# Two pieces of the last x sums formed two half parts later, two blocks of output sums held aside, all products of half part 1 ahead of its tiles

## The chip, the core and the metric

The kernel runs on one core of a Trainium2 chip. The metric is the device time of one execution in microseconds (us). Five engines run side by side and wait for one another by semaphores: TensorE (PE, with its weight loads shown as PEld), VectorE (DVE), ScalarE (ACT), GpSimd (POOL) and SyncE (SP), which here issues all DMA transfers in its program order. Each engine executes its instructions in order.

## What is computed

```python
attn_out = _attn_ref(**attn_kwargs)
x = np.ascontiguousarray(attn_out.transpose(0, 2, 1, 3)).reshape(B * S, H * D)
x = _moe_ref(x=x, **moe_kwargs)
return _moe2_ref(x=x, **moe2_kwargs)

def _moe2_ref(x, w_in, w_out):          # x 2304 x 512, w_in 512 x 2048, w_out 2048 x 512
    h = x @ w_in
    g = np.where(h > 0.0, h, np.exp(np.minimum(h, 0.0)) - 1.0)
    return (g @ w_out).astype(np.float32)
```

An attention with local windows and global tokens feeds a mixture of eight experts, all of which run on all tokens and are weighted by a Sinkhorn-normalised gate. Its output x feeds a last network of two layers with an ELU between them. The change lies where the experts end and the last network begins.

## The kernel before

**Numbers.** Each fp32 operand is held as a high part and a low part (names ending in h and l, or hh and hl for the hidden values). One product of two operands is three matmuls: high by high, low by high, high by low.

**Token groups.** The 2304 tokens go through the experts in two groups, p = 0 (1024 tokens) and p = 1, and through the last network in the same two groups, there called p = 2 and p = 3. The nine blocks `accs[0]` to `accs[8]` (128 x 512 fp32 each) collect the expert output of a group. For the first group they are stored and read back early. For the second group they still hold the expert output when the last network begins, and from then on `part2` uses the same blocks for the outputs of the last network.

**Layer one** is done with seven products instead of eight (Strassen's scheme in Winograd's form). Its operands on the x side are four blocks and four sums of blocks, called 11, 12, 22, s1 to s4 here. `x_pair(p, j, rows)` forms them for a piece j of a group: TensorE transposes two blocks of `accs` into two PSUM tiles x2t (`turned`), ScalarE and VectorE form high and low parts (`hi`, `lo`, with four stores to the scratch tensors xo3h and xo3l), then the sums (`first`, `second`) and their high and low parts (`hi_sums`, `lo_sums`, with two more stores). For the second group there are five pieces, formed in the order 1, 0, 2, 3, 4. Piece j reads `accs[j]` and `accs[j + 4]`, piece 4 only `accs[8]` and is half as large. The tiles for the high and low parts have the tags s1, u2 and u3, each with two buffers that are used in turn.

**The same tags serve the products.** `Quad.product` runs one of the seven products (1 to 7); a product is six matmuls. Products 1, 6 and 7 keep a partial result in SBUF under the tags s1 (ScalarE copy, L1064), u2 and u3 (VectorE add, L1066). Products 2, 3, 4 and 5 end in `evac` (VectorE add, t, L1018) and then `elu`: three ScalarE activations (L1036 to L1038), two VectorE operations (eg, L1041 and L1042), a ScalarE cast that gives the high part hh (L1054) and a GpSimd subtraction that gives the low part hl (L1055). Product 3 is accumulated into the PSUM bank of product 5 of the same half part after that bank has been read.

**Half parts.** The last network runs in 16 half parts, eight for each group, called 0 to 15 here. Each has the products of one half of a 512-wide piece of the hidden layer, mixed with the tiles of layer two of the half part before. A tile (`part2`, also six matmuls, two per low or high part of each of two hidden chunks) adds to one block of `accs`. The order inside a half part is a string: a1 is product 1 of quad a, b1 of quad b, z3 product 3 of the half part before, t4 tile 4 of the half part before. Half part 0 runs `TURN_0`, 1 runs `TURN_1`, 2 to 7 run `TURN_A`, 8 (where the group changes) runs `TURN_AB`. Tiles 4 to 7 of a half part need the results of its products 5 and 4, tiles 0 to 3 those of its products 2 and 3.

**What sets the order.** The scheduler is off, so program order is issue order on each engine. `side2` is a queue of small steps; a fixed number (`per`) is taken from it after every tile of the experts' last part (`mix2_all`) or every element of a half part's string. Before the change the last part of the experts takes pieces 1, 0 and 2 from it, five steps after each tile, and half part 0 takes pieces 3 and 4, three steps after each product. Between the two, `layer_two(0, f)` issues eight loads of the layer-two weights (w2h, w2l), which wait until the experts' last tile has read the old ones. `layer_one` loads the weights wh and wl.

**Raw tiles.** `raw_tile` gives one of four large SBUF buffers in turn; each piece of the x sums takes two (xsr, xsh).

Of the kernel before, what the change touches and what calls it, by code (L numbers as in the profile page):

```python
# [47 lines left out]
XUSE = ("11", "s2", "12", "s3", "s1", "22")  # L48
W22 = ("11", "t2", "21", "t3", "t1", "t4", "22")
TURN_0 = "a1 a6 a2 a7 a5 a4"  # L50
TURN_1 = "a1 a6 a2 z3 a7 t4 a5 t5 a4 t6 t7 t0 t1 t2 t3"
TURN_A = "a1 a6 t4 a2 t5 z3 t6 a7 t7 a5 a4 t0 t1 t2 t3"
TURN_AB = "a1 a6 t4 a2 t5 z3 t6 a7 a5 t7 a4 b1 t0 b6 b2 t1 a3 t2 b7 t3 b5 b4"
TURN_B = "a1 a6 t0 a2 t1 z3 t4 a7 a5 t5 a4 b1 t6 b6 b2 t7 a3 t2 b7 t3 b5 t8 b4"
TURN_END = "z3 t0 t1 t4 t5 t6 t7 t8 t2 t3"

# [4 lines left out]
def tile_net(ctx: ExitStack, tc, kq, vw, vc, qg, wg, w1, w2, wi, wo, consts, out):  # L61
# [602 lines left out]
    def raw_tile(shape, dt, name):  # L664
        r = rawm.tile([128, 2 * HALF], F32, tag="raw", name=name)
        n = int(np.prod(shape))
        v = r[:, :n].bitcast(dt)
        return v.rearrange("p (a f) -> p a f", a=shape[0])
# [197 lines left out]
    def x_pair(p, j, rows):  # L866
# [31 lines left out]
                nc.sync.dma_start(xo[p, q][:, 6:8, c], g.bitcast(F32))  # L898

        def first():  # L900
            t = s["s"] = raw_tile((8, n), F32, "xsr")
            nc.scalar.copy(t[:, 6:8], s[2][:, :2])
            comb(t[:, 4:6], s[1][:, :2], t[:, 6:8], ALU.subtract)
            comb(t[:, 0:2], s[2][:, 2:], t[:, 6:8], ALU.add)
# [4 lines left out]
            comb(t[:, 6:8], s[1][:, 2:], t[:, 2:4], ALU.subtract)  # L909

        def hi_sums():
            s["k"] = raw_tile((8, n), F32R, "xsh")
            nc.scalar.copy(s["k"], s["s"])

        def lo_sums():
# [6 lines left out]
    def operands(p, names, c0, c1):  # L922
        for n in names:
            for q in "hl":
                nc.sync.dma_start(xop[n + q][:, :, c0:c1].bitcast(F32), xo[p, q][:, 2 * XORDER.index(n):2 * XORDER.index(n) + 2, c0:c1])
# [221 lines left out]
        rests()  # L1147
        return quads[-1]

    def mix2_all(p, u, last):  # L1150
        tiles = TP[p] // 128
        if p == 0:
            pre, mid = [(i, (0, 2)) for i in (4, 5, 6)], []
            rest = [(i, (1, 3)) for i in (4, 5, 6)] + [(7, range(4))]
        else:
            pre, mid, rest = [(0, range(4))], [], [(i, range(4)) for i in ((1, 5, 4, 6, 2, 7, 3, 8) if u == U1 - 1 else (1, 5))]
        seen = {i for i, _ in pre + mid + rest}
        rest += [(i, range(4)) for i in range(tiles) if i not in seen]
        for i, f in pre:
            mix2(p, u, i, f)  # L1160
        last.product(3)
        per = -(-len(side2) // (len(mid) + len(rest) - 1))
        for i, f in mid + rest:
            mix2(p, u, i, f)
            rests()
            pop(side2, per)

    with tc.manual_schedule():
# [30 lines left out]
        for a, ((p, u), after) in enumerate(zip(order, order[1:])):  # L1199
# [32 lines left out]
            if not moe:  # L1232
                at[1, 3] = lambda: operands(2, (*XUSE, "s4"), 0, HALF // 2)
                at[2, 3] = lambda: layer_one(0, 0)
                first = [lambda: operands(2, XUSE, HALF // 2, SL), lambda: layer_one(0, 1, W22[:-1])]
                side2.extend([lambda: operands(2, ("s4",), HALF // 2, SL), lambda: layer_one(0, 1, W22[-1:])] + 8 * [None])
                xs_ = [x_pair(3, j, lambda j=j: (accs[j], accs[j + 4])) for j in (1, 0, 2, 3)]
                xs_.append(x_pair(3, 4, lambda: (accs[8],)))
                side2.extend(xs_[0] + xs_[1] + xs_[2])
                side2.extend([None] * (35 - len(side2)))  # L1240
            elif switch:
                first = [lambda: second_x(("11", "s2", "12", "s3", "s1", "22"))]
                side2.append(lambda: second_x(("s4",)))
# [3 lines left out]
                f()  # L1247
            if moe:
                side2.extend(b1 + end + between + ld2 if a in BACK else b1 + ld2 + end)
            mix2_all(p, u, last)  # L1250
            pop(side2, len(side2))
            if switch and moe:
                for i in range(TP[0] // 128):
# [2 lines left out]
        def rows_of(p, q, fc, i):  # L1256

            c = i * 128 if p == 2 or i < 4 else SL if i == 8 else (i + 1) * 128
            return hs[q][:, fc, c:c + 128]

        def part2(p, u, f, i):

            ps = psum.tile([128, 512], F32, tag="b", name="m2")
            for fc in (f, f + 2):
                h, l = (rows_of(p, q, fc, i) for q in "hl")
                for _ in three(ps, h, l, w2s["h"][:, fc], w2s["l"][:, fc], fc == f, fc > f):
                    passed(227.0)
            if (p, u, f) in ((2, 0, 0), (3, U2 - 1, 0)):
                nc.vector.tensor_copy(accs[i], ps)
            else:  # L1270
                nc.vector.tensor_tensor(out=accs[i], in0=ps, in1=accs[i], op=ALU.add)  # L1271
            if (p, u, f) in ((2, U2 - 1, 1), (3, 0, 1)):
                j = i + (p - 2) * TP[0] // 128
                if j < LOC // 128:
                    r0 = (j // 4) * (SL + SG) + SG + 128 * (j % 4)
                    nc.sync.dma_start(out[r0:r0 + 128, :], accs[i])
                else:
                    for b in range(B):
                        r0 = b * (SL + SG)
                        nc.sync.dma_start(out[r0:r0 + SG, :], accs[i][SG * b:SG * b + SG, :])  # L1280

        turns = [(2, u, f) for u in range(U2) for f in range(2)]
        turns += [(3, u, f) for u in range(U2)[::-1] for f in range(2)]
# [9 lines left out]
        for k in range(len(turns) + 1):  # L1293
# [6 lines left out]
                seq = TURN_B if turns[k - 1][0] == p else TURN_AB  # L1300
                quads = [Quad(3, g0, HALF // 2, f, HALF) for g0 in (0, HALF // 2)]
            seq = seq.split()
            if k == 0:
                side2.extend(xs_[3] + xs_[4])
            per = -(-len(side2) // len(seq))
            for e in seq:
                w, i = e[0], int(e[1])
# [94 lines left out]
```

## Time and profile before

| | us |
|---|---|
| median of 3 runs | 2011.12 (2011.08 to 2013.51) |
| the profiled execution | 2012.12 |
| its span, first to last instruction | 2010.3 |
| TensorE busy in the span | 1971.1 (98%) |
| VectorE, ScalarE, GpSimd busy | 1521.4, 815.8, 761.6 |
| mean granted clock of TensorE | 0.993 of full speed |

The profile is of one execution; it is 1.0 us above the median. Matmuls follow one another before the one ahead has ended, so the distance from start to start is what a matmul costs, and a bracket behind a row of the timeline gives the idle time ahead of it and what ended it. The granted clock is either full (2.4 GHz) or half (1.2 GHz); a mean between 0.5 and 1 over a stretch mixes the two.

### The profile page before, as it was taken

The page shows a single profiled execution, that of the slowest core. Times are in us where ns is not written, and L with a number is a line of the kernel's source. Part 1 is how long each engine was busy: PE and PEld are TensorE (multiplying, and loading weights), DVE is VectorE, ACT ScalarE, POOL GpSimd, SP SyncE. Part 2 cuts the span into 40 slices and gives each one's busy share as a digit, 9 for nine tenths or more (in the row PEclk, how much of TensorE's full clock was granted, in tenths as well). Part 3 has the DMA queues.
Part 4 walks back from the last instruction along what each step waited for, and adds up shares of the span by engine and source line. Part 5 has one row for each costly group of instructions (what it writes and reads, how often), then busy time and mean ns, then how long its engine had stood idle before and what let it go on. Part 6 is the DMA issues. An engine that isn't in the chain of part 4 may idle for free. (4 is left out here: it accounts for less than half of the span.)

```text
span 2010.3 us, 30549 instructions
## 1 busy us (share of the span) xinstructions
PE 1971.1 (98%) x11099; PEld 1719.9 (86%) x11099; DVE 1521.4 (76%) x2840; ACT 815.8 (41%) x1683; POOL 761.6 (38%) x665
## 2 busy tenths in 40 slices
PE   8999899999999999999999999999999969999999
PEld 7998887888888888899999999999999957778998
DVE  7777767776777767778878787888888667778887
ACT  6655524332333333333333333333333234545664
POOL 7565513333232323324354353545455102222322
PEclk9999999999999999999999999999999989999999
DMA  7446451223322232443333434333233594555432
GB/s 233 138 129 198 132 203 53 74 66 102 116 87 97 72 111 78 173 148 99 121 95 116 122 117 130 109 107 103 91 100 100 172 273 130 151 188 157 119 116 69
DMA packets 204518, 251.01 MB, mean 125 GB/s; under 512 B 17232, under 2 KB 150096, under 8 KB 204368
## 3 DMA queue, kind: packets, MB, share of 16 engines
q1 hardware_dynamic: 204368, 249.06, 39.1%
q8 instruction: 87, 1.43, 0.3%
q14 instruction: 63, 0.52, 0.1%
HBM read 190.16 MB, written 58.85 MB: 124 GB/s over the span
## 5 line engine op out<-in xcount | busy, mean ns | idle before, releaser
L131 PE MATMUL m<-w2h,hh 128*128 128x512 f32 x1360 | 533.8, 392 | 8.2 <-ACT hh L1054 8.2
L135 PE MATMUL m<-w2h,hl 128*128 128x512 f32 x1360 | 535.5, 394 | 1.4 <-POOL hl L1055 1.2
L133 PE MATMUL m<-w2l,hh 128*128 128x512 f32 x1360 | 533.5, 392 | 0.0
L1024 ACT ACTIVATE hh<-t 128x288 fp32r<-128x288 f32 (+1 forms) x368 | 184.8, 502 | 433.0 <-DVE t L1018 429.0
L135 PEld LDWEIGHTS m<-w2h,hl 128*128 128x128 f32 x1360 | 255.6, 188 | 58.5 <-POOL hl L1055 6.4
L131 PEld LDWEIGHTS m<-w2h,hh 128*128 128x128 f32 x1360 | 255.8, 188 | 56.8 <-ACT hh L1054 8.8
L133 PEld LDWEIGHTS m<-w2l,hh 128*128 128x128 f32 x1360 | 255.8, 188 | 49.3
L1026 DVE SCALAR_TENSOR_TENSOR hl<-t,hh 128x288 fp32r<-128x288 f32 (+1 forms) x368 | 282.2, 767 | 4.0 <-ACT hh L1024 0.2
L127 POOL TENSOR_TENSOR w2l<-w2r,w2h 128x512 fp32r<-128x512 f32 x120 | 163.7, 1388 | 299.0 <-ACT w2h L123 272.1
L1126 DVE SCALAR_TENSOR_TENSOR acc<-m,pr,acc 128x512 f32<-128x512 f32 x247 | 183.2, 746 | 109.8 <-PE m L135 108.3
L1018 DVE TENSOR_TENSOR t<-q,u 128x288 f32<-128x288 f32 (+1 forms) x348 | 182.9, 527 | 62.4 <-PE q L1085 52.8
L1055 POOL TENSOR_TENSOR hl<-eg,hh 128x288 fp32r<-128x288 f32 (+2 forms) x112 | 101.7, 915 | 310.6 <-ACT hh L1054 230.2
L743 ACT CAST wh<-wt 128x512 fp32r<-128x512 f32 x120 | 68.9, 619 | 235.0 <-POOL wt L739 235.0
L739 POOL TENSOR_TENSOR wt<-w1r,wt 128x512 f32<-128x512 f32 x60 | 89.1, 1485 | 194.3 <-DVE hl L1026 101.7
L739 POOL TENSOR_TENSOR wt<-w1r 128x512 f32<-128x512 f32 x60 | 79.9, 1335 | 166.5 <-DVE hl L1026 124.2
L1066 DVE TENSOR_TENSOR u<-q,s 128x288 f32<-128x288 f32 (+1 forms) x116 | 61.2, 528 | 84.5 <-PE q L1085 62.7
L747 DVE TENSOR_TENSOR wl<-wt,wh 128x512 fp32r<-128x512 f32 x120 | 107.2, 904 | 12.8 <-ACT wh L743 11.0
L1271 DVE TENSOR_TENSOR acc<-m,acc 128x512 f32<-128x512 f32 x119 | 81.2, 687 | 35.6 <-PE m L135 35.4
L813 POOL TENSOR_TENSOR cp<-r,cp 128x512 f32<-128x512 f32 x32 | 42.6, 1332 | 144.3 <-DVE cp L803 75.8
L253 ACT ACTIVATE e<-s,m 128x192 f32<-128x192 f32 (+1 forms) x128 | 55.8, 437 | 79.8 <-DVE m L245 79.2
L1083 PE MATMUL q<-xs4h,wh 128*128 128x288 f32 (+1 forms) x232 | 75.9, 327 | 10.4 <-DVE t L1018 10.4
L316 PEld LDWEIGHTS o<-vw,pt 112*128 112x128 f32 x512 | 76.7, 193 | 9.1 <-issue 3.9
(243 smaller groups left out, 4682.1 us busy)
## 6 DMA issues: line engine op xcount, KB each, us to landing
w1r<-in_w_dram SPq DMA_DIRECT2D x60, 512.0 KB, 5.1
w2r<-in_w_dram SPq DMA_DIRECT2D x60, 512.0 KB, 4.1
kq<-in_kq_dram SPq DMA_DIRECT2D x31, 544.0 KB, 4.2
wh<-wqh SPq DMA_DIRECT2D x98, 128.0 KB, 2.6
wl<-wql SPq DMA_DIRECT2D x98, 128.0 KB, 2.6
r<-in_wo_dram SPq DMA_DIRECT2D x16, 512.0 KB, 4.0
r<-in_wi_dram SPq DMA_DIRECT2D x16, 512.0 KB, 4.3
vw<-in_vw_dram SPq DMA_DIRECT2D x32, 227.5 KB, 4.7
```

The costliest lines, as they stand in the source:

```text
L127: e.tensor_tensor(out=lo, in0=src, in1=hi.bitcast(F32), op=ALU.subtract)
L131: nc.tensor.matmul(ps, ah, bh, start=first, stop=False)
L133: nc.tensor.matmul(ps, ah, bl, start=False, stop=False)
L135: nc.tensor.matmul(ps, al, bh, start=False, stop=last)
L739: eng.tensor_tensor(out=t, in0=get(a), in1=get(b), op=op)
L747: eng.tensor_tensor(out=wop[n + "l"], in0=src, in1=wop[n + "h"].bitcast(F32), op=ALU.subtract)
L1018: nc.vector.tensor_tensor(out=t, in0=ps, in1=rest, op=ALU.add)
L1024: nc.scalar.activation(hh, t, AF.Relu)
L1026: late.append(lambda: nc.vector.scalar_tensor_tensor(out=hl, in0=t, scalar=0.0, in1=hh.bitcast(F32), op0=ALU.max, op1=ALU.subtract))
L1055: nc.gpsimd.tensor_tensor(out=hl, in0=g[:, a:b], in1=hh.bitcast(F32), op=ALU.subtract)
L1126: nc.vector.scalar_tensor_tensor(out=accs[i], in0=ps, scalar=scale, in1=accs[i], op0=ALU.mult, op1=ALU.add)
L1271: nc.vector.tensor_tensor(out=accs[i], in0=ps, in1=accs[i], op=ALU.add)
```

## The change

- Pieces 3 and 4 of the second group's x sums leave half part 0. Piece 3 is formed in half part 2 and piece 4 in half part 3, one step after each element of the string, beginning behind z3.
- `accs[3]` and `accs[7]` therefore have to keep the expert output until half part 2. Tiles 3 and 7 of the first group add into a raw tile of their own instead (`aside`), for the whole of group p = 2, and the output is stored from there.
- Since `aside` occupies one of the four raw tiles, piece 4 puts its sums and their high parts into one raw tile of 16 rows.
- The last part of the experts takes four steps after each tile instead of five, with pauses (None) that put each piece's transposes one tile later than before; it has 32 steps, so the last four stand behind the last tile.
- `TURN_1` has all seven products first, then the eight tiles. `TURN_AB` has a1, a6, a2 and z3 ahead of t4 and t5, and t0 behind b6.

```diff
-TURN_1 = "a1 a6 a2 z3 a7 t4 a5 t5 a4 t6 t7 t0 t1 t2 t3"
+TURN_1 = "a1 a6 a2 z3 a7 a5 a4 t4 t5 t6 t7 t0 t1 t2 t3"
-TURN_AB = "a1 a6 t4 a2 t5 z3 t6 a7 a5 t7 a4 b1 t0 b6 b2 t1 a3 t2 b7 t3 b5 b4"
+TURN_AB = "a1 a6 a2 z3 t4 t5 a7 t6 a5 t7 a4 b1 b6 t0 b2 t1 a3 t2 b7 t3 b5 b4"
...
-            t = s["s"] = raw_tile((8, n), F32, "xsr")
+            s["r"] = raw_tile((8 if j < 4 else 16, n), F32, "xsr")
+            t = s["s"] = s["r"][:, :8]
...
-            s["k"] = raw_tile((8, n), F32R, "xsh")
+            s["k"] = raw_tile((8, n), F32R, "xsh") if j < 4 else s["r"][:, 8:].bitcast(F32R)
...
-        per = -(-len(side2) // (len(mid) + len(rest) - 1))
+        per = per or -(-len(side2) // (len(mid) + len(rest) - 1))
...
-                side2.extend([lambda: operands(2, ("s4",), HALF // 2, SL), lambda: layer_one(0, 1, W22[-1:])] + 8 * [None])
+                side2.extend([lambda: operands(2, ("s4",), HALF // 2, SL), lambda: layer_one(0, 1, W22[-1:])] + 6 * [None])
...
-                side2.extend(xs_[0] + xs_[1] + xs_[2])
-                side2.extend([None] * (35 - len(side2)))
+                s0, s1, s2 = xs_[:3]
+                side2.extend([*s0[:3], None, *s0[3:6], None, s0[6], *s1[:3], *s1[3:6], None, s1[6], *s2])
...
-            mix2_all(p, u, last)
+            mix2_all(p, u, last, 0 if moe else 4)
...
+        aside = raw_tile((2, 512), F32, "yr")
...
+            acc = aside[:, i // 4] if p == 2 and i % 4 == 3 else accs[i]
...
-            if k == 0:
-                side2.extend(xs_[3] + xs_[4])
+            if k in (2, 3):
+                s = xs_[k + 1]
+                side2.extend([None] * 5 + s[:5] + [None, s[5], None, s[6]])
```

In `part2` every use of `accs[i]` becomes `acc`. Nothing is added or removed in sum: the same matmuls, transposes, VectorE, ScalarE and GpSimd instructions and the same transfers are issued.

VectorE in half part 0, before: from the high and low parts of piece 3 (xu2 and xu3 of x2t_16252) to the result of product 5. u2 and u3 on the left without x are the partial results of the products.

```order
L890 TENSOR_TENSOR xu3_16263<-x2t_16253,xu3_16263 128x256
L1066 TENSOR_TENSOR u2_16280<-q6_16273,s1_16250 128x512
L890 TENSOR_TENSOR xsr_16282<-x2t_16252,xsr_16282 128x256
L890 TENSOR_TENSOR xsr_16282<-x2t_16253,xsr_16282 128x256
L890 TENSOR_TENSOR xsr_16282<-xsr_16282,x2t_16252 128x256
L890 TENSOR_TENSOR xsr_16282<-x2t_16252,xsr_16282 128x256
L1018 TENSOR_TENSOR t_16297<-q2_16290,s1_16250 128x512
L890 TENSOR_TENSOR xsr_16282<-xsr_16282,xsh_16288 128x1024
L1066 TENSOR_TENSOR u3_16323<-q7_16316,u2_16280 128x512
L890 TENSOR_TENSOR xu2_16325<-x2t_16307,xs1_16312 128x256
```

After, from the last steps of piece 2 to the result of product 4:

```order
L890 TENSOR_TENSOR xsr_16224<-xsr_16224,x2t_16189 128x256
L890 TENSOR_TENSOR xsr_16224<-x2t_16189,xsr_16224 128x256
L890 TENSOR_TENSOR xsr_16224<-xsr_16224,xsh_16230 128x1024
L1067 TENSOR_TENSOR u2_16260<-q6_16253,s1_16251 128x512
L1019 TENSOR_TENSOR t_16269<-q2_16262,s1_16251 128x512
L1067 TENSOR_TENSOR u3_16283<-q7_16276,u2_16260 128x512
L1019 TENSOR_TENSOR t_16292<-q5_16285,u3_16283 128x512
L1042 SCALAR_TENSOR_TENSOR eg_16272<-eg_16272,er_16271 128x512
L1043 SCALAR_TENSOR_TENSOR eg_16272<-t_16269,eg_16272 128x512
L1019 TENSOR_TENSOR t_16308<-q4_16301,u3_16283 128x512
```

The steps of pieces 3 and 4 are gone from between the products' results, and the rest of piece 2 (sums and low parts) stands ahead of all of them.

TensorE in half part 1, before: from product 7 to product 4 (m2_16453 is tile 4, m2_16481 tile 5).

```order
L1085 MATMUL q7_16442<-xs3h_3782,wl_102 128x512
L131 MATMUL m2_16453<-w2h_105,hh_103 128x512
L133 MATMUL m2_16453<-w2l_106,hh_103 128x512
L135 MATMUL m2_16453<-w2h_105,hl_104 128x512
...
L1083 MATMUL q5_16465<-xs1h_3778,wh_101 128x512
L1084 MATMUL q5_16465<-xs1l_3779,wh_101 128x512
L1085 MATMUL q5_16465<-xs1h_3778,wl_102 128x512
...
L131 MATMUL m2_16481<-w2h_105,hh_103 128x512
L133 MATMUL m2_16481<-w2l_106,hh_103 128x512
L135 MATMUL m2_16481<-w2h_105,hl_104 128x512
```

After, from product 7 to tile 4 (m2_16441):

```order
L1086 MATMUL q7_16384<-xs3h_3782,wl_102 128x512
L1084 MATMUL q5_16395<-xs1h_3778,wh_101 128x512
L1085 MATMUL q5_16395<-xs1l_3779,wh_101 128x512
L1086 MATMUL q5_16395<-xs1h_3778,wl_102 128x512
...
L1084 MATMUL q4_16413<-x22h_97,wh_101 128x512
L1085 MATMUL q4_16413<-x22l_98,wh_101 128x512
L1086 MATMUL q4_16413<-x22h_97,wl_102 128x512
...
L131 MATMUL m2_16441<-w2h_105,hh_103 128x512
L133 MATMUL m2_16441<-w2l_106,hh_103 128x512
L135 MATMUL m2_16441<-w2h_105,hl_104 128x512
```

Tile 4, the first reader of half part 0's hidden values, moved behind two products.

TensorE in half part 8, before: from product 6 to product 3 of the half part before (xs4, accumulated in q5). m2_17655 and m2_17678 are tiles 4 and 5.

```order
L1085 MATMUL q6_17646<-xs2h_3780,wl_102 128x288
L131 MATMUL m2_17655<-w2h_105,hh_103 128x512
L133 MATMUL m2_17655<-w2l_106,hh_103 128x512
L135 MATMUL m2_17655<-w2h_105,hl_104 128x512
...
L1085 MATMUL q2_17664<-x12h_95,wl_102 128x288
L131 MATMUL m2_17678<-w2h_105,hh_103 128x512
L133 MATMUL m2_17678<-w2l_106,hh_103 128x512
L135 MATMUL m2_17678<-w2h_105,hl_104 128x512
L1083 MATMUL q5_17565<-xs4h_99,wh_101 128x512
```

After, from product 6 to tile 4 (m2_17684):

```order
L1086 MATMUL q6_17646<-xs2h_3780,wl_102 128x288
L1084 MATMUL q2_17655<-x12h_95,wh_101 128x288
...
L1086 MATMUL q2_17655<-x12h_95,wl_102 128x288
L1084 MATMUL q5_17565<-xs4h_99,wh_101 128x512
L1085 MATMUL q5_17565<-xs4l_100,wh_101 128x512
L1086 MATMUL q5_17565<-xs4h_99,wl_102 128x512
...
L131 MATMUL m2_17684<-w2h_105,hh_103 128x512
L133 MATMUL m2_17684<-w2l_106,hh_103 128x512
L135 MATMUL m2_17684<-w2h_105,hl_104 128x512
```

Product 2 and product 3 moved ahead of tiles 4 and 5.

## Rows read from the trace of the kernel before

**Rows 1.** The page's first part: busy us, share of the span, instructions of TensorE

```profile
PE 1971.1 (98%) x11099; PEld 1719.9 (86%) x11099; DVE 1521.4 (76%) x2840; ACT 815.8 (41%) x1683; POOL 761.6 (38%) x665
```

**Rows 2.** Waits of TensorE from 1600 us to the end: total, times, longest

```profile
PE q L1083 <- DVE t L1018: 10.4, 1, 10.4
PE m L131 <- ACT hh L1054: 8.2, 1, 8.2
PE m L135 <- POOL hl L1055: 1.2, 3, 0.7
PE x2t L876 <- DVE acc L1126: 1.1, 1, 1.1
```

**Rows 3.** Windows: us, busy PE PEld DVE ACT POOL, clock, DMA; half parts 1, 3

```profile
1634.48:1677.77 43.29, 24.58 (x91) 18.84 (x91) 28.31 (x41) 19.38 (x34) 8.96 (x7) 0.76 0.68 201
...
1698.63:1719.50 20.87, 20.73 (x90) 16.37 (x89) 16.16 (x23) 10.22 (x17) 5.62 (x5) 1.00 0.47 138
```

**Rows 4.** Timeline of TensorE in half part 1: start, duration, line, tile, idle before

```profile
1638.35 0.39 PE L1085 MATMUL q<-x12h,wl 128*128 128x512 f32 x1
1649.09 0.80 PE L1083 MATMUL q<-xs4h,wh 128*128 128x512 f32 x1 [10.35 <-DVE t L1018]
...
1652.93 0.39 PE L1084 MATMUL q<-xs3l,wh 128*128 128x512 f32 x1
1653.16 0.40 PE L1085 MATMUL q<-xs3h,wl 128*128 128x512 f32 x1
1661.71 0.80 PE L131 MATMUL m<-w2h,hh 128*128 128x512 f32 x1 [8.16 <-ACT hh L1054]
...
1665.86 0.40 PE L1085 MATMUL q<-xs1h,wl 128*128 128x512 f32 x1
```

**Rows 5.** Timeline of VectorE: the partial result u3 of half part 0

```profile
1645.75 0.69 DVE L1066 TENSOR_TENSOR u<-q,u 128x512 f32<-128x512 f32 x1 [8.37 <-DMA xo3l<-xu]
```

**Rows 6.** Timeline of SP: u3 stores of pieces 0, 2, 3; first layer-two load

```profile
1623.86 0.46 SPq L898 DMA_DIRECT2D xo3l<-xu  x1
...
1629.88 0.71 SPq L898 DMA_DIRECT2D xo3l<-xu  x1
...
1632.26 1.38 SPq L937 DMA_DIRECT2D w2h<-wdh  x1
...
1640.80 0.74 SPq L898 DMA_DIRECT2D xo3l<-xu  x1
```

**Rows 7.** DMA issues, 1570 to 1672 us: count, KB each, median us to landing

```profile
w2h<-wdh SPq DMA_DIRECT2D x4, 256.0 KB, 5.3
```

**Rows 8.** Timeline of ScalarE in half part 3: three ELU activations, then a cast

```profile
1716.50 0.62 ACT L1036 ACTIVATE er<-t 128x512 f32<-128x512 f32 x1
...
1718.41 0.61 ACT L1054 CAST hh<-eg 128x512 fp32r<-128x512 f32 x1
```

**Rows 9.** Timeline of VectorE, same time: the second ELU operation twice

```profile
1717.42 0.69 DVE L1042 SCALAR_TENSOR_TENSOR eg<-t,eg 128x512 f32<-128x512 f32 x1
...
1719.35 1.66 DVE L1042 SCALAR_TENSOR_TENSOR eg<-t,eg 128x512 f32<-128x512 f32 x1
```

**Rows 10.** Timeline of GpSimd, same time: two low parts of hidden values

```profile
1719.16 1.30 POOL L1055 TENSOR_TENSOR hl<-eg,hh 128x512 fp32r<-128x512 f32 x1 [3.72 <-ACT hh L1054]
1721.81 1.29 POOL L1055 TENSOR_TENSOR hl<-eg,hh 128x512 fp32r<-128x512 f32 x1 [1.35 <-ACT hh L1054]
```

**Rows 11.** Windows, line L890 alone: VectorE's busy time for piece 3's operations

```profile
1631.50:1637.60 6.10, 3.84 (x7) 1.00 0.96 276
```

**Rows 12.** Timeline of TensorE in half part 8: waits of tiles 4 and 0

```profile
1805.97 0.40 PE L133 MATMUL m<-w2l,hh 128*128 128x512 f32 x1
1807.05 0.50 PE L135 MATMUL m<-w2h,hl 128*128 128x512 f32 x1 [0.69 <-POOL hl L1055]
...
1819.24 0.49 PE L135 MATMUL m<-w2h,hl 128*128 128x512 f32 x1 [0.35 <-POOL hl L1055]
```

More of the change, by code (lines that the diff above doesn't have):

```diff
@@ L1148, in mix1, with mix2_all @@
         return quads[-1]
-    def mix2_all(p, u, last):
+    def mix2_all(p, u, last, per=0):
         tiles = TP[p] // 128
@@ L1268, in part2 @@
             if (p, u, f) in ((2, 0, 0), (3, U2 - 1, 0)):
-                nc.vector.tensor_copy(accs[i], ps)
+                nc.vector.tensor_copy(acc, ps)
             else:
-                nc.vector.tensor_tensor(out=accs[i], in0=ps, in1=accs[i], op=ALU.add)
+                nc.vector.tensor_tensor(out=acc, in0=ps, in1=acc, op=ALU.add)
             if (p, u, f) in ((2, U2 - 1, 1), (3, 0, 1)):
@@ L1275, in part2 @@
                     r0 = (j // 4) * (SL + SG) + SG + 128 * (j % 4)
-                    nc.sync.dma_start(out[r0:r0 + 128, :], accs[i])
+                    nc.sync.dma_start(out[r0:r0 + 128, :], acc)
                 else:
@@ L1279, in part2 @@
                         r0 = b * (SL + SG)
-                        nc.sync.dma_start(out[r0:r0 + SG, :], accs[i][SG * b:SG * b + SG, :])
+                        nc.sync.dma_start(out[r0:r0 + SG, :], acc[SG * b:SG * b + SG, :])
         turns = [(2, u, f) for u in range(U2) for f in range(2)]
```

## Prediction

> **What bounds the kernel now.** I read the page first: TensorE is busy 98% of the span [rows 1], so only time in which it stands still or runs slowly can be won; everything else lies beside it. The waits of TensorE come next. From 1600 us on there are four kinds, 20.9 us together, and two single waits are nearly all of it [rows 2]. The windows say where: half part 1 takes 43.29 us at a mean clock of 0.76, half part 3 with the same products and tiles 20.87 us at full clock [rows 3]. The timeline of TensorE shows what the extra 22 us are made of. After product 2 of half part 1 it waits 10.35 us for z3, comes back at half speed, does product 7, waits 8.16 us for tile 4, and comes back at half speed again [rows 4]. Behind the first wait stands VectorE, which at 1645.75 had been idle for 8.37 us until a store from tile xu had landed [rows 5]: u3 of half part 0 needs the buffer that piece 3 had filled, and SP issued piece 3's last u3 store at 1640.80 only, behind piece 2's stores and the layer-two loads [rows 6]. Without u3 there is no result of product 5, so its bank is not read and z3 can't accumulate into it. The second wait is the ELU chain of half part 0, which started late for the same reason.
>
> **What the change takes away.** A full-speed matmul step is 1653.16 - 1652.93 = 0.23 us, a product or tile of six 1.39 [rows 4].
> First wait: 1649.09 - 1638.35 less one step = 10.5. Half speed after it: ten steps to 1652.93 take 3.84 instead of 2.30: 1.5. Second wait: 1661.71 - 1653.16 less one step = 8.3. From 1661.71 to 1665.86 eight steps take 4.15 instead of 1.84, partly waiting for hl: 2.3 [rows 4]. Transposes of piece 2: they now come one tile after the accumulation that they read, so that wait of 1.1 goes [rows 2]. Half part 8: tile 4 comes two products later (0.8 for product 2 at half width and 1.4 for z3), more than its third matmul waits, 1807.05 - 1805.97 less 0.23 = 0.85; tile 0 comes two tiles and one short product further behind z3, more than its 0.35 [rows 12]. With the slower first step after each wait (some 0.1 each, twice): 1.4.
> Sum: 10.5 + 1.5 + 8.3 + 2.3 + 1.1 + 1.4 = 25.1 us.
>
> **Why the first wait really goes.** The three tags have two buffers in turn. Pieces 1, 0 and 2 fill buffers A, B and A; half part 0 now takes B, piece 0's, and half part 1 takes A, piece 2's. SP issued piece 0's last u3 store at 1623.86 [rows 6]; with the slow landing of 5.3 that the layer-two loads show at that time [rows 7] it is free by 1629.2. Half part 0 starts 1.2 earlier than before, at 1623.7, so product 7 ends at 1623.7 + 4 x 1.39 = 1629.3. Nothing is lost there. Piece 2's buffer is free by 1629.88 + 5.3 = 1635.2, and half part 1's product 7 ends at 1638.8. The layer-two loads start no earlier than before, at 1632.26, and those that tile 4 reads were issued by 1636; they land by about 1641.
>
> **What is late next.** This is the term with the widest bounds. Tile 4 of half part 1 is due after 13 products, at 1623.7 + 13 x 1.39 = 1641.8. It needs hh and hl of product 4 of half part 0. From 1623.9 VectorE adds tile 8 (0.7) and does piece 2's sums and their low parts, about 2.8 of the 3.84 that a whole piece takes [rows 11], with a cast of about 1.1 on ScalarE between them, which ends at about 1628.6. Then come u2 and t of product 2, so ScalarE starts the first ELU at about 1630.1. On ScalarE stand from there to product 4's hh: four groups of three activations at 1.91, three casts of 0.61 and one copy of about 0.6 [rows 8], 10.1 together, and two gaps: eg of product 4 takes the buffer of product 2's and waits for GpSimd's 1.3 [rows 10], some 0.9; and the fourth group waits for VectorE, which itself waits for the copy, 2.2 to 2.8. So hh comes at about 1643.3 to 1643.9 and hl 1.4 later. The first matmul of tile 4 waits 1.5 to 2.1, the third 0.9 more. I take 2.8, with bounds 0 (the gaps overlap) and 8 (below). z3's own ELU ends about when tile 0 needs it: 0.2.
>
> **Pieces 3 and 4 in half parts 2 and 3.** Their transposes move and cost nothing new. VectorE gets 3.8 us more in half part 2 [rows 11] and somewhat over half of it, 2.4, in half part 3, since piece 4 is half as wide; before, both lay beside the first wait. There is room in sum, 20.87 - 16.16 = 4.7 [rows 3], but not at every place: they stand ahead of the results of products 5 and 4, and of the end of that chain depends tile 4 of the next half part. In half part 3 the low part of product 4 ran from 1721.81 to 1723.10 [rows 10], and tile 4 of half part 4, two products after its start, needs it within 0.2 us of that; there is no slack. I follow the order: t of product 4 moves by 2.5 us less what VectorE idled there, hl by about 1.5 to 2. I take 1.0 for half part 2 and 0.8 for half part 3, with bounds 0 and 3 each. The stores of both pieces fall into stages with a DMA share of 0.47 [rows 3] and cost nothing.
> The Trainium skill (GPSIMD Engine Reference, Specifications) says that GpSimd shares its SBUF interfaces with VectorE and contends with VectorE instructions that have two SBUF inputs. The trace agrees: the same L1042 took 0.69 alone and 1.66 beside hl [rows 9, 10]. The moved subtraction of piece 3 has two SBUF inputs; by that rule it would be about 1 us longer beside hl, and the sum 1 us smaller.
>
> **The sum.** 25.1 - 2.8 - 0.2 - 1.0 - 0.8 = 20.3 us. The profiled execution took 2012.12 and would take 1991.8; it lies 1.0 above the median of 2011.12, so I forecast a median of 1990.8.
>
> **Rivals.**
> *All waits vanish:* if ScalarE's gaps overlap and VectorE's room suffices, 25.1 is kept: 1986.0. For it speaks that in half parts 2 to 7, which have the same chain in the same order, no wait of tile 4 for hh is listed [rows 2]; against it, the chain above has no slack. Chance 0.13.
> *The late chain:* if u3 of half part 0 still follows stores, now those of piece 2, it comes at 1635.2 instead of 1630.0, everything in the ELU chain 5 us later, and tile 4 waits some 8 instead of 2.8. A wait of that length came back at half speed, one of 1.1 did not [rows 2, 4], so 2.3 are added: gain 20.3 - 5.2 - 2.3 = 12.8, time 1998.3. The change then does only half of what it says. The Trainium skill (TensorE: Matmul & The Clock Gate, "Why this matters for your kernels") says the same of idle gaps between bursts, that they bring the slow clock back; no row here shows which way one of 2.8 falls, and at half speed the forecast would be 1993. Chance 0.22 for 1994 to 2000.
> *VectorE becomes the bound, slower than before:* from half part 2 on VectorE has 16.16 + 3.8 = 20.0 of 20.87 [rows 3, 11]. If operations with two SBUF inputs are each held as in the slow row (+1.0, [rows 9]) one or more of them already takes it past 20.87 and it falls behind; to undo the gain it has to stay behind by 3.4 us at the start of each of the six half parts 2 to 7 (6 x 3.4 = 20.4): 2011 to 2014. Against it: from half part 4 on no piece is left, and 4.7 us of room in each drains the backlog. Chance 0.03, and 0.02 for something in between.
>
> **How the numbers follow.** The forecast, 1987.5 to 1994, has 0.60. The range of 1985.5 to 1998.5 takes in the bound with all waits gone and the late chain up to its worked-out time and leaves out about 0.12. A measurement of this kernel can tell 0.2%, 4 us, from no change. Faster by more than that is every case but the last: 0.95. Same 0.02, slower 0.03.
>
> **What would show it.** In the profile after: half part 1 without a wait of more than 1 us for t at z3, and all at full clock; VectorE's u3 of half part 0 at about 1630 with no wait for a DMA; a wait of tile 4 for hh (L1055 there) of 1 to 3 us; small waits for hl at tile 4 of half parts 3 and 4; none in half part 8; the transposes x2t without a wait for acc. I am wrong if TensorE shows a mean clock well below 1 in half part 1, or waits in half parts 2 to 4 that sum to over 4 us.

## The result, and the profile after

The changed kernel takes **1992.78 us** (median of 4 runs, 1992.23 to 1993.08), the kernel before, beside it on the same chip, 2011.48. The ratio is 0.9905, with a 95% interval of 0.9888 to 0.9922: 0.95% faster, 18.7 us. The forecast was 1990.8 in a range of 1985.5 to 1998.5. The profiled execution took 1992.23 (span 1990.4) against 2012.12 before: 19.9 us, where the sum had 20.3.

TensorE stays the bound. The page's first part of the changed kernel answers to [rows 1]: TensorE has 4.1 us less busy time, 2.3 of it in half part 1, where fewer of its steps run slowly, and a span shorter by 19.9.

```profile
PE 1967.0 (99%) x11099; PEld 1717.9 (86%) x11099; DVE 1516.8 (76%) x2840; ACT 815.2 (41%) x1683; POOL 763.4 (38%) x665
```

The waits of TensorE from 1590 us to the end, after (what waited, for whom, total us, times, longest), answer to [rows 2]. The 10.4 us of z3 for t and the 1.1 us of the transposes are gone, the 8.2 us of tile 4 have become 2.2, and hl has grown from 1.2 to 2.3.

```profile
PE m L135 <- POOL hl L1056: 2.3, 3, 1.4
PE m L131 <- ACT hh L1055: 2.2, 1, 2.2
```

Two windows of the changed kernel, half parts 1 and 3 (length, busy PE, PEld, DVE, ACT, POOL, granted clock, DMA share, GB/s), answer to [rows 3]; the second ends 1.3 us before its half part does. Half part 1 has lost 18.4 us and is nearly at full clock.

```profile
1631.91:1656.81 24.90, 22.26 (x91) 17.55 (x90) 21.86 (x25) 14.87 (x26) 8.67 (x7) 0.93 0.94 275
...
1678.42:1700.00 21.58, 20.19 (x90) 16.14 (x89) 17.06 (x28) 10.80 (x20) 6.10 (x4) 1.00 0.67 194
```

From the starts of the half parts (first matmul of product 1 on TensorE's timeline) in both traces follows where the 19.9 us went. Half part 0 starts 1.21 earlier.

| half part | before, us | after, us | gain |
|---|---|---|---|
| 0 | 9.57 | 8.21 | 1.36 |
| 1 | 43.29 | 24.90 | 18.39 |
| 2 | 20.86 | 21.61 | -0.75 |
| 3 | 21.32 | 22.88 | -1.56 |
| 4 | 20.98 | 21.55 | -0.57 |
| 5 to 7 | 62.93 | 63.03 | -0.10 |
| 8 to the end of the span | 206.44 | 204.52 | 1.92 |

The gain of half part 0 is the transposes of pieces 3 and 4, which half parts 2 and 3 now carry. Nearly all the rest is half part 1, and what is left to gain there is tile 4. TensorE's timeline of the changed kernel there (start, duration, line, operation; in brackets the idle time before it and who ended it):

```profile
1641.20 0.39 PE L1086 MATMUL q<-x22h,wl 128*128 128x512 f32 x1
1643.74 0.51 PE L131 MATMUL m<-w2h,hh 128*128 128x512 f32 x1 [2.15 <-ACT hh L1055]
1644.08 0.59 PE L133 MATMUL m<-w2l,hh 128*128 128x512 f32 x1
1645.17 0.80 PE L135 MATMUL m<-w2h,hl 128*128 128x512 f32 x1 [0.49 <-POOL hl L1056]
1645.76 0.63 PE L131 MATMUL m<-w2h,hh 128*128 128x512 f32 x1
1646.19 0.63 PE L133 MATMUL m<-w2l,hh 128*128 128x512 f32 x1
...
1647.73 0.40 PE L135 MATMUL m<-w2h,hl 128*128 128x512 f32 x1
...
1648.65 0.39 PE L131 MATMUL m<-w2h,hh 128*128 128x512 f32 x1
```

From 1641.20 to 1648.65 are 13 steps, 2.96 us at full speed; they took 7.45, so tile 4 costs **4.5 us**: 2.3 until hh is there, 0.9 until hl, 1.3 in slower steps, most of them 0.43 instead of 0.23.

### The profile page after: what moved, and what is told of

It reads as the page before. It is cut to its first block, busy times and chain, and to the rows that moved or that the text cites. A ratio compares the mean times of both kernels' runs of the same rounds, so it can differ in the third digit from the quotient of the medians.

```text
span 1990.4 us, 30550 instructions
## 1 busy us (share of the span) xinstructions
PE 1967.0 (99%) x11099; PEld 1717.9 (86%) x11099; DVE 1516.8 (76%) x2840; ACT 815.2 (41%) x1683; POOL 763.4 (38%) x665
## 5 line engine op out<-in xcount | busy, mean ns | idle before, releaser
L1275 DVE TENSOR_TENSOR acc<-m,acc 128x512 f32<-128x512 f32 x105 | 72.1, 687 | 33.3 <-PE m L135 33.2
L316 PE MATMUL o<-vw,pt 112*128 112x65 f32 x512 | 78.0, 259 | 5.4 <-issue 3.4
```

Of the source, the lines that this page charges most:

```text
L316: nc.tensor.matmul(s["o"][:, i, :], pt[:, (i % 2) * 2 + j, :], s["v"][:, i, j, :], start=(j == 0), stop=(j == 1))
```

## The experiments

The kernels of the experiments ran in three sets, each on a chip of its own, beside the kernel before, which took 2012.15 to 2013.17 there and 2011.48 beside the changed kernel. A difference of under 2 us from the changed kernel's median therefore counts only where the traces show the same.

**Both parts apart.** The first kernel has the pieces back in half part 0 and keeps the new orders.

```
-            if k in (2, 3):
-                s = xs_[k + 1]
-                side2.extend([None] * 5 + s[:5] + [None, s[5], None, s[6]])
+            if k == 0:
+                side2.extend(xs_[3] + xs_[4])
```

> The changed kernel, with pieces 3 and 4 of the sums back in half part 0; the new orders of half parts 1 and 8, the missing pauses and the aside tile stay. Theory (piece 3's stores hold the buffer that u3 of half part 0 takes): u3 waits again about 8 us for a store, z3 waits about 10 us for t, TensorE comes back at half speed, and tile 4 of half part 1 still waits some 5 to 7 us for its ELU. That is 10 + 1.5 + 6 less the 4.5 that tile 4 loses in the changed kernel: about 13 us more, 2004 to 2008. Rival (the new orders and the missing pauses carry the gain): within 2 us of the changed kernel, 1991 to 1995, and no wait over 3 us in half parts 0 and 1.

It took 2008.73 us (2006.95 to 2009.29; ratio to before 0.9977, 0.9968 to 0.9987), 16 over the changed kernel by the medians and 14.7 by the spans of the profiles: a little more than the 13 expected, and 0.7 above the upper end of 2004 to 2008. TensorE's two main waits and the start of u3 of half part 0 on VectorE in this kernel:

```profile
PE q L1084 <- DVE t L1019: 10.5, 1, 10.5
PE m L131 <- ACT hh L1055: 5.2, 1, 5.2
```

```profile
1644.99 0.69 DVE L1067 TENSOR_TENSOR u<-q,u 128x512 f32<-128x512 f32 x1 [8.50 <-DMA xo3l<-xu]
```

The stall of [rows 4, 5] is back with both its parts, 8.50 instead of 8.37 us long at u3; the second part is 5.2 and not 8.2, since the new order asks for tile 4 later. The theory holds; the rival, that the orders carry the gain, falls.

The second kernel moves the pieces alone, with the old orders.

```
-TURN_1 = "a1 a6 a2 z3 a7 a5 a4 t4 t5 t6 t7 t0 t1 t2 t3"
+TURN_1 = "a1 a6 a2 z3 a7 t4 a5 t5 a4 t6 t7 t0 t1 t2 t3"
-TURN_AB = "a1 a6 a2 z3 t4 t5 a7 t6 a5 t7 a4 b1 b6 t0 b2 t1 a3 t2 b7 t3 b5 b4"
+TURN_AB = "a1 a6 t4 a2 t5 z3 t6 a7 a5 t7 a4 b1 t0 b6 b2 t1 a3 t2 b7 t3 b5 b4"
```

> The changed kernel with the old orders of half parts 1 and 8: the two pieces moved alone. Theory (the two parts add up): no wait of z3; tile 4 of half part 1 is due two products earlier while its hh comes at the same time, so it waits 2.15 + 2.8 = about 5 us and more of what follows runs at half speed: 2.8 more; in half part 8 the 1.9 us that the new order gave come back: 1997 to 1998.5. Rival (the orders are worth nothing once the pieces are gone): no more than 1 us over the changed kernel, 1992 to 1994.

It took 1998.17 us (1997.25 to 1999.21; ratio 0.9929, 0.9914 to 0.9943), 5.4 over the changed kernel, as the theory had it. The waits of TensorE:

```profile
PE m L131 <- ACT hh L1055: 4.9, 1, 4.9
PE m L135 <- POOL hl L1056: 3.0, 5, 1.4
```

Half part 1 takes 28.44 us instead of 24.90, 3.5 more, and from half part 8 to the end of the span 206.47 instead of 204.52, 1.95 more: together the 5.4 that the runs show. So the pieces alone give 0.71%, the orders (with the pauses ahead of the transposes) without them 0.23%, each within 0.15; the two sum to 0.94%, and the whole change gave 0.95%. The parts add up.

**Which buffer.** The prediction blamed one buffer, that of u3. In the kernel before, two stores of piece 3 were made to read other tiles of the same size, so that the u3 buffer comes free without them; bytes, queue and work of the engines stay. What this kernel leaves out is the right values in two of the sums of that piece.

```
-                nc.sync.dma_start(xo[p, q][:, 6:8, c], g.bitcast(F32))
+                nc.sync.dma_start(xo[p, q][:, 6:8, c], (g if j != 3 else t[:, :2]).bitcast(F32))
```

> The kernel before, with one thing changed: the two stores of piece 3 that read its u3 tile read the s1 and u2 tiles instead. The same number of bytes goes through the same queue at the same place, and VectorE and ScalarE do the same work; only the u3 buffer is free once VectorE has written it. (Two of the sums of one piece then hold other values, which changes no time.) Theory (the buffer): VectorE no longer waits 8.4 us at u3, the 10.4 us wait of z3 falls to under 3, and the half speed behind it goes with it; tile 4 of half part 1 stays some 5 to 8 us late, since its due time moves up with its chain. Gain 8 to 13 us: 1998 to 2003. Rival (the load of two pieces on VectorE, ScalarE and the transfers in that stage makes half part 0 late): the wait of z3 stays above 7 us, and the time within 3 us of the kernel before, 2008 to 2014.

It took 2012.42 us (2010.44 to 2013.26; ratio 0.9997, 0.9987 to 1.0006): no gain. The theory's number was missed, and the time is the one that the rival, the load of the two pieces, had named. VectorE's timeline in this kernel:

```profile
1637.61 0.68 DVE L1066 TENSOR_TENSOR u<-q,u 128x512 f32<-128x512 f32 x1
1645.98 0.42 DVE L890 TENSOR_TENSOR xu<-x2t,xs 128x256 fp32r<-128x256 f32 x1 [7.69 <-DMA xo3l<-xu]
```

u3 came 8.1 us earlier than in [rows 5], without a wait. But the next instruction on VectorE, piece 4's low part, writes the u2 buffer that piece 3's stores read too, and waits as long; t of product 5, which z3 needs, stands behind it. Then the u2 buffer was freed as well, with all four of these stores reading the s1 tile.

```
-            for q, t, g in (("h", s["h"], s["g"][:, :2]), ("l", s["l"], s["g"][:, 2:])):
+            g0, l0 = (s["g"], s["l"]) if j != 3 else (s["h"], s["h"])
+            for q, t, g in (("h", s["h"], g0[:, :2]), ("l", l0, g0[:, 2:])):
```

> The kernel before, with all four stores of piece 3 that read its s1, u2 and u3 tiles reading the s1 tile: same bytes, same queue, same places, and both xu buffers free once VectorE has written them. (Some of the sums of one piece then hold other values.) In the run with u3 alone freed, u3 of half part 0 came at 1637.61 without a wait, but the next instruction on VectorE, piece 4's low part, waited 7.69 us for the u2 buffer that the same stores hold, and t of product 5 behind it came no earlier. Theory (buffers held by the stores, in VectorE's order): now t of product 5 comes 7 to 8 us earlier, the wait of z3 falls from 10 to 3 or less, and its half speed goes; tile 4 stays 5 to 8 us late: 2001 to 2005. Rival (something else of the pieces holds VectorE or ScalarE): another wait of some 8 us in the same place, time 2009 to 2014.

It took 2004.72 us (2004.31 to 2007.53; ratio 0.9965, 0.9952 to 0.9978), within the forecast. The waits of TensorE, and t of product 5 on VectorE:

```profile
PE m L131 <- ACT hh L1055: 9.2, 1, 9.2
PE q L1084 <- DVE t L1019: 1.8, 1, 1.8
```

```profile
1639.71 0.68 DVE L1019 TENSOR_TENSOR t<-q,u 128x512 f32<-128x512 f32 x1
```

VectorE's t of product 5 came at 1639.71 instead of 1648.35, and z3 waited 1.8 instead of 10.4. So the first wait is due to piece 3's stores holding two buffers, and not to the load that the pieces put on VectorE or the queues, which is unchanged here. The u2 buffer alone was enough for the whole stall; that the u3 buffer alone would be is seen from [rows 5], not from a run with u2 freed alone. Two details of the theory failed: the half speed behind z3 did not go, though the wait was only 1.8, and tile 4 is 9.2 us late, not 5 to 8, because its due time comes forward with the chain. Only the new place of the pieces and the new order together remove most of that.

**Why tile 4 still waits.** Product 2 of half part 0, whose ELU only tile 0 needs, was put last.

```
-TURN_0 = "a1 a6 a2 a7 a5 a4"
+TURN_0 = "a1 a6 a7 a5 a4 a2"
```

> The changed kernel, with product 2 of half part 0 last (order 1 6 7 5 4 2), so that the ELUs of products 5 and 4, which tile 4 of half part 1 reads, come first and that of product 2, which only tile 0 needs, third. Theory (the late ELU chain is what tile 4 waits for, and the half speed behind it is due to the wait): hh of product 4 comes one group, 2.5 to 3 us, earlier, at about 1640.5; the 2.15 us wait goes, hl keeps at most 0.5, no matmul of tile 4 takes 0.43 instead of 0.23, and all or nearly all of the 4.5 us lost there comes back: 1988 to 1989.5. Rival (tile 4 is held by the layer-two loads, which end at about 1641 to 1643 too): the wait stays at 1 to 2 us with a transfer as what ends it, gain under 2: 1991 to 1993.

It took 2012.43 us and says nothing on tile 4. Behind product 4 the kernel issues the loads of the next weights into the same operands, so product 2 now read the weights of a later half part and waited for them:

```profile
PE q L1084 <- DMA wh<-wqh: 15.1, 1, 15.1
```

With those loads issued behind product 2 the question could be put.

```
-                    if i == 4 and q is quads[-1]:
+                    if i == (4 if k else 2) and q is quads[-1]:
```

> As the run with product 2 last in half part 0, but with the loads of the next weights issued behind product 2 and not behind product 4. (In that run product 2 read the weights of a later half part and waited 15.1 us for their loads, so it says nothing on tile 4.) Theory (the late ELU chain is what tile 4 waits for, and the half speed behind it is due to the wait): hh of product 4 comes 2.5 to 3 us earlier, at about 1640.5; the 2.15 us wait goes, hl keeps at most 0.5, all matmuls of tile 4 run at full speed, and all or nearly all of the 4.5 us lost there comes back: 1988 to 1989.5. Rival (tile 4 is held by the layer-two loads, which land at about 1642 too): the wait stays at 1 to 2 us with a transfer at its end, gain under 2: 1991 to 1993.

It took 1994.68 us (1993.93 to 1995.67; ratio 0.9911, 0.9897 to 0.9926), 1.9 more than the changed kernel, where the theory had 3 to 5 less. Tiles 4 to 7 do start on time, but tile 0, which comes behind them, then waits:

```profile
PE m L131 <- ACT hh L1055: 3.4, 1, 3.4
PE m L135 <- POOL hl L1056: 2.7, 3, 1.3
```

The rival, layer-two loads that land late, falls too: tile 4 began at 1641.25 with no wait.

```profile
1641.25 0.39 PE L131 MATMUL m<-w2h,hh 128*128 128x512 f32 x1
```

The reason stands in ScalarE's and VectorE's timelines of the changed kernel. VectorE first:

```profile
1639.85 0.69 DVE L1043 SCALAR_TENSOR_TENSOR eg<-t,eg 128x512 f32<-128x512 f32 x1
1640.45 0.69 DVE L1019 TENSOR_TENSOR t<-q,s 128x512 f32<-128x512 f32 x1
```

```profile
1637.28 0.62 ACT L1055 CAST hh<-eg 128x512 fp32r<-128x512 f32 x1
1641.17 0.63 ACT L1037 ACTIVATE er<-t 128x512 f32<-128x512 f32 x1 [3.27 <-DVE t L1019]
...
1643.09 0.60 ACT L1055 CAST hh<-eg 128x512 fp32r<-128x512 f32 x1
```

The input of product 4's hh was complete at 1639.85 + 0.69 = 1640.54. ScalarE was idle, but the next instruction in its order was the first activation for half part 1's own product 2, whose t came last on VectorE. It waited 3.27 us for it, did three activations, and made hh at 1643.09, 2.5 us after it could have. The prediction had this wait in its sum, as 2.2 to 2.8, but took the order as given. In the run with product 2 last the same three activations stand ahead of product 2's own hh, and tile 0 pays.

So one cast was moved: while product 2 of half part 1 is set up, all casts still outstanding are issued first. Nothing else in the order of any engine changes.

```
-            while sum(e[2] for e in stages) > 1:
+            while sum(e[2] for e in stages) > most[0]:
...
+                most[0] = 0 if k == 1 and e in ('a2',) else 1
```

> The changed kernel with one step moved: in half part 1, ScalarE makes hh of product 4 (the ELU that tile 4 waits for) ahead of the ELU activations of half part 1's own product 2. In the changed kernel its input was complete at 1640.54, but ScalarE stood 3.27 us behind a first activation whose t came at 1641.14 and made hh only at 1643.09. Theory (tile 4 waits for hh because of this order on ScalarE, not because the chain of ELUs is full): hh starts at about 1640.6, 2.5 us earlier, hl 1.3 after it; tile 4 starts without a wait for hh, its third matmul waits at most 0.8 for hl, all its steps take 0.23; 3 to 4 us come back there, of which up to 1.5 go again at tile 0, whose hl of product 3 then comes last: 1989 to 1991. Rival (the chain of ELUs is full, and the wait only moves to other tiles, as in the run with product 2 last): within 1 us of the changed kernel, 1992 to 1994.

It took 1990.72 us (1990.66 to 1991.42; ratio 0.9893, 0.9876 to 0.9909), 2.1 less than the changed kernel by the medians and near the upper end of 1989 to 1991. ScalarE, the waits of TensorE, and half part 1 in a window:

```profile
1640.83 0.62 ACT L1055 CAST hh<-eg 128x512 fp32r<-128x512 f32 x1 [2.67 <-DVE eg L1043]
1641.43 0.63 ACT L1037 ACTIVATE er<-t 128x512 f32<-128x512 f32 x1
```

```profile
PE m L135 <- POOL hl L1056: 3.3, 4, 1.4
PE m L131 <- ACT hh L1055: 0.4, 1, 0.4
```

```profile
1632.17:1655.29 23.12, 21.29 (x92) 16.66 (x90) 20.35 (x25) 14.99 (x26) 8.21 (x6) 1.00 0.98 288
```

hh comes 2.3 us earlier, tile 4 starts at once and waits 0.55 for hl; half part 1 runs at full clock and takes 23.12 us instead of 24.90, 1.8 less. The 0.4 and 0.9 of what is left now stand at tile 0, for hh and hl of product 3, as the theory had it. Then z3 was set two products earlier as well, with the cast ahead of its ELU.

```
-TURN_1 = "a1 a6 a2 z3 a7 a5 a4 t4 t5 t6 t7 t0 t1 t2 t3"
+TURN_1 = "a1 z3 a6 a2 a7 a5 a4 t4 t5 t6 t7 t0 t1 t2 t3"
...
+                most[0] = 0 if k == 1 and e in ('z3',) else 1
```

> The changed kernel with hh of product 4 ahead as in the run before this one, and z3 two products earlier in half part 1 (1 z3 6 2 7 5 4), so that the last ELU of half part 0 comes ahead of half part 1's own on VectorE and ScalarE. Theory: tile 4 as in that run, and hh and hl of product 3 come 2 to 3 us earlier than there, so tile 0 waits for nothing: the whole 4 us come back, 1988 to 1990. Rival (VectorE and ScalarE are late by as much whatever their order): no better than the run with hh ahead alone, 1990 to 1992.

It took 1988.68 us (1987.76 to 1989.29; ratio 0.9881, 0.9866 to 0.9896), within the 1988 to 1990 expected. Its only waits, and half part 1 in a window, without a gap:

```profile
PE m L135 <- POOL hl L1056: 1.9, 2, 1.4
```

```profile
1632.61:1653.06 20.45, 20.45 (x91) 16.89 (x90) 18.34 (x24) 14.71 (x26) 8.43 (x6) 1.00 0.96 289
```

Half part 1 takes 4.45 us less than in the changed kernel, which is the cost of tile 4 worked out above. VectorE and ScalarE have the same instructions to do, so their order was at fault and not their number. VectorE's busy time in the half part fell too, from 21.86 us to 18.34.

**What the low clock costs.** Ten matmuls on loaded operands fill the gap ahead of tile 4 in the changed kernel; the first real product overwrites what they leave.

```
+            if (p, u, f, i) == (2, 0, 0, 4):
+                x = xop["s2h"]
+                for _ in range(10):
+                    nc.tensor.matmul(ps, x[:, 0, :128], x[:, 0, :512], start=True, stop=True, skip_group_check=True)
```

> The changed kernel, with ten matmuls of 128x512 on loaded operands into tile 4's own bank ahead of tile 4 of half part 1; its first real product overwrites them. They fill the 2.15 us in which TensorE stood still there and do nothing else. Theory (TensorE's slow steps of 0.43 behind the wait are a lower clock that follows from standing still, about 8 steps of 0.2): all steps of tiles 4 and 5 take 0.23, tile 4 starts at the same time, and 1.2 to 1.7 us come back: 1991.0 to 1991.7. Rival (those steps were waits for hl or for operands that the trace doesn't list): the steps stay at 0.43 and the time at 1992.5 to 1993.

TensorE's timeline of this kernel:

```profile
1640.32 2.43 PE L1271 MATMUL m<-xs2h 128*128 128x512 f32 x10
1642.64 0.50 PE L131 MATMUL m<-w2h,hh 128*128 128x512 f32 x1
...
1644.06 0.50 PE L135 MATMUL m<-w2h,hl 128*128 128x512 f32 x1 [0.68 <-POOL hl L1056]
...
1645.09 0.40 PE L131 MATMUL m<-w2h,hh 128*128 128x512 f32 x1
...
1650.81 0.50 PE L135 MATMUL m<-w2h,hl 128*128 128x512 f32 x1 [0.34 <-POOL hl L1056]
```

Tile 4 starts 11.84 us after its half part, as in the changed kernel (11.83), and the steps behind it take 0.23, but for the wait of 0.68 for hl and the first step after each stop (0.34). The slow steps were the clock, then, and a consequence of standing still; the rival falls. Tile 6 starts 1.1 us earlier, a little under the 1.2 to 1.7 expected. But tile 0 then finds hl of product 3 not ready and gives 0.5 back, so the half part ends 0.44 earlier. The time of 1991.99 (1990.75 to 1993.76; ratio 0.9901, 0.9884 to 0.9917) lies 0.3 above the forecast of 1991.0 to 1991.7 and can't be told from that of the changed kernel.

**The pieces in half parts 2 and 3.** They were spread differently, their cast behind product 5's hh.

```
-                side2.extend([None] * 5 + s[:5] + [None, s[5], None, s[6]])
+                side2.extend([None] * 3 + s[:5] + [None] * 4 + [s[5], None, s[6]])
```

> The changed kernel, with pieces 3 and 4 spread differently over half parts 2 and 3: transposes two places earlier, the cast and the low parts of the sums two places later, behind the ELU of product 5. Theory (in half part 2 the pieces' operations stand ahead of the results of products 5 and 4 on VectorE, and their cast of 1.03 us ahead of the last two hh on ScalarE): hl of product 4 comes 1 to 2 us earlier, the 1.39 us wait of tile 4 of half part 3 and the 0.40 of half part 4 fall to 0.5 together or less: 1 to 1.5 us less, 1990.5 to 1992. Rival (these waits come from hh and hl themselves, GpSimd beside VectorE, wherever the pieces stand): the two waits stay at 1.4 and 0.4, time 1992 to 1993.5.

It took 1992.29 us (1992.01 to 1993.20; ratio 0.9900, 0.9884 to 0.9917). The wait of tile 4 of half part 3 fell from 1.39 to 0.66, but a tile of half part 2 now waits 0.26 for hl, and half parts 2 to 4 together take 66.10 us instead of 66.04. The waits behind it:

```profile
PE m L131 <- ACT hh L1055: 2.1, 1, 2.1
PE m L135 <- POOL hl L1056: 1.9, 4, 0.7
```

Neither theory nor rival is quite right. The first wait fell, as the theory had it and against the rival; but others took its place, and what the pieces cost there stays, as the rival had it for the time. Half part 1, which this edit leaves alone, took 25.43 us instead of 24.90: behind the same wait of 2.15 more steps were slow. So half a microsecond there, as in the run with the gap filled, is no more than it varies by. The same edit on top of the kernel with z3 early:

> The run with z3 early and hh ahead, and pieces 3 and 4 spread over half parts 2 and 3 as in the run of that. Theory (the two are independent): the 0.5 us that the spread took from the waits of tile 4 of half parts 3 and 4 come on top, 1987.5 to 1989.5. Rival: no difference from the run with z3 early, or up to 1 us more, 1989 to 1991.

It took 1988.30 us (1987.92 to 1988.65; ratio 0.9880, 0.9865 to 0.9894), which is the fastest here and can't be told from 1988.68. Its four runs lie 3.6 to 5.2 us under those of the changed kernel; the two were not run side by side, and by the ratios to before their intervals overlap. Half parts 2 to 4 take 66.44 us here and 66.36 in the run with z3 early alone: the spread is worth nothing on top either, and the rival holds.

## Why the prediction was right, point by point

**The first wait** (10.5 and 1.5 of half speed). It is gone as forecast, and u3 of half part 0 came at 1629.69, forecast about 1630, with no transfer ahead of it:

```profile
1629.69 0.68 DVE L1067 TENSOR_TENSOR u<-q,u 128x512 f32<-128x512 f32 x1
```

The place was right and the cause half told: the prediction named one buffer, and the stores held two that VectorE needs one after the other. The change frees both at once, so the sum was not touched by that; a change that had freed the named one alone would have gained nothing. (Its 1638.8 for the end of product 7 of half part 1 is 1639.0 by its own 1.39; nothing hangs on it.)

**The second wait** (8.3 and 2.3) and its successor (2.8). The working had hh at 1643.3 to 1643.9; it ended at 1643.69. But the term was taken too small: the 1.5 to 2.1 for the first matmul was 2.3, as tile 4 was due at 1641.4 and not 1641.8 (a product took 1.36, not 1.39), the 0.9 for the third was 0.9, and the half speed behind it was left out, 1.3. That is **4.5 against 2.8**, the largest miss, inside the bounds of 0 and 8. The prediction had said that no row showed whether a wait of 2.8 brings the low clock. A wait of 2.15 did. The Trainium skill (TensorE: Matmul & The Clock Gate, "Why this matters for your kernels") says that idle gaps between bursts bring the slow clock back; this row agrees in kind, and the filled gap shows it from the other side, but the Trainium skill names gaps longer than this one, and here 2.15 was enough. The prediction's 1993 for that case lies beside the measured 1992.8 in part by luck: it took 2.3 for the half speed, which cost 1.3. The claim that the chain above has no slack was wrong in kind: the work has slack, ScalarE's order had none. With that order changed, half part 1 ran without a wait and the time was 1988.7; the rival in which all waits vanish had 1986.0.

**Transposes of piece 2** (1.1). Their wait is gone, in this kernel and in all with its code up to there. Half part 0 starts 1.21 earlier, but this pair of profiles alone would not show it: in those kernels it starts anywhere from 1622.6 to 1625.3.

**Half part 8** (1.4). It gave 1.9; none of its tiles waits now, and with the old order the whole of it came back. For tile 0 the prediction took the bracket, 0.35; from start to start, as for tile 4, the wait is 0.5.

**Pieces in half parts 2 and 3** (1.0 and 0.8). The timeline of TensorE in half parts 3 and 4, tile 4's third matmul:

```profile
1683.21 0.50 PE L135 MATMUL m<-w2h,hl 128*128 128x512 f32 x1 [1.39 <-POOL hl L1056]
...
1705.10 0.50 PE L135 MATMUL m<-w2h,hl 128*128 128x512 f32 x1 [0.40 <-POOL hl L1056]
```

With the slower step behind each they cost 1.7 and 0.7. By the table, half parts 2 to 4 lost 2.9 in all; 1.4 of it is the transposes that half part 0 no longer has. VectorE was busy for 17.1 us of 21.6 in half part 2 and 18.4 of 22.9 in half part 3, so it never became the bound, and the third rival falls. The subtraction that was moved beside hl took 1.93 instead of the 1.23 that piece 2's takes in half part 0: 0.7 longer, where the prediction had about 1 by the Trainium skill (GPSIMD Engine Reference, Specifications), which has GpSimd and VectorE contend for SBUF. The prediction put this price on VectorE alone. TensorE waited for GpSimd, and there the two hl beside that subtraction took 3.50, where two by themselves take 2.6 (1.30 each):

```profile
1680.10 1.93 DVE L890 TENSOR_TENSOR xsr<-xsr,xsh 128x1024 fp32r<-128x1024 f32 x1
```

```profile
1679.65 3.50 POOL L1056 TENSOR_TENSOR hl<-eg,hh 128x512 fp32r<-128x512 f32 x2 [6.32 <-ACT hh L1055]
```

That is 0.9 more, ahead of the hl that tile 4 waited for; how much of the 1.39 it makes, no run separates.

**The signs.** Of what the prediction said would show it, all came but one: half part 1 is not all at full clock, its mean is 0.93 (0.76 before). A mean well below 1 there was also its sign of being wrong. The missing part stands behind tile 4, not behind z3.

**The sum.** With the measured terms it is 25.1 + 0.5 - 4.5 - 1.7 - 0.7 = 18.7, and the profiled execution gained 19.9; of the remaining 1.2, 0.5 are waits of 0.4 and 0.1 that half parts 3 and 4 had before, and the rest is not resolved. The errors of tile 4 (-1.7), half part 3 (-0.7), half part 8 (+0.5) and two smaller ones (z3's 0.2, which did not come, and 0.1 in half part 4) make -1.6, and the 1.2 that no term held makes up for most of it: that 20.3 lies so near to 19.9 is partly luck. The median was missed by 2.0, since the prediction took the profiled execution to lie 1.0 above it again, and it lay 0.55 below. The rival of a late chain got its clock right and its cause wrong: nothing followed a store.

## What to carry to other kernels

A wait for a buffer can hide a wait for another: before freeing one, read the next instructions of the same engine and ask what they would wait for. Where a consumer waits for the last step of a chain, look at when that step's input was complete and what its engine had queued ahead of it; moving one cast of 0.6 us was worth 1.8 us of half part 1 here, and with one product moved too, 4.45. And add to the price of a gap on TensorE the slow steps after it, 1.1 to 1.8 us here, but count them as won only as far as the next operand is there in time.

## What the runs showed of the hardware

TensorE fell to half its clock behind waits of 1.85, 2.15, 3.41, 4.86 us and more. It kept the full clock behind waits of 0.55 and 0.90 (half part 1 of the kernel with one cast moved) and 1.39 (half part 3 of the changed kernel). Behind the gap of 2.15 the granted clock was 0.53 and then 0.62 of full speed:

```profile
1644.00:1646.00 2.00, 1.51 (x4) 0.78 (x4) 1.99 (x2) 1.05 (x3) 1.11 (x1) 0.53 1.18 296
1646.00:1648.00 2.00, 2.00 (x7) 1.52 (x7) 1.69 (x3) 1.48 (x3) 0.97 (x1) 0.62 1.15 292
```

Behind the shorter of these waits the low clock didn't hold from the first step on: after 2.15 the first matmul's step was still 0.34, as after waits without a fall of the clock, and later ones were 0.43; after 1.85 us, in the kernel with both buffers freed, four steps passed before the first of 0.42. After 4.86 the first step was already 0.59. Nor do equal waits cost the same: the slow steps behind 2.15 cost 1.3 us in the changed kernel and 1.8 in the one with the pieces spread differently. The timeline of the kernel with both buffers freed:

```profile
1640.44 0.50 PE L1084 MATMUL q<-xs4h,wh 128*128 128x512 f32 x1 [1.85 <-DVE t L1019]
1640.78 0.39 PE L1085 MATMUL q<-xs4l,wh 128*128 128x512 f32 x1
...
1641.55 0.63 PE L1085 MATMUL q<-xs4l,wh 128*128 128x512 f32 x1
1641.97 0.63 PE L1086 MATMUL q<-xs4h,wl 128*128 128x512 f32 x1
```
